# Moving VectorE's small SBUF operations of a kernel's first part to GpSimd, ScalarE and scalar operands

## The chip, the cores and the metric

The kernel runs on one core of a Trainium2 chip. The metric is the time of one execution on the device in microseconds (us). A core has engines that run their own instruction queues in order and wait for one another by semaphores: TensorE (PE, with its weight loads PEld), VectorE (DVE), ScalarE (ACT) and GpSimd (POOL); SyncE (SP) issues all of this kernel's DMA transfers from one queue.

## What is computed

```python
# attention over keys and values pooled by 8, 8 batches x 8 heads x 576 x 64
k_p = k.reshape(B, H, Sp, pool, D).mean(axis=3)
v_p = v.reshape(B, H, Sp, pool, D).mean(axis=3)
scores = scale * np.matmul(q, k_p.transpose(0, 1, 3, 2))
scores = scores - np.max(scores, axis=-1, keepdims=True)
attn = np.exp(scores)
attn = attn / (np.sum(attn, axis=-1, keepdims=True) + 1e-09)
x = np.matmul(attn, v_p)
# first layer, 4608 tokens, 512 -> 1024 -> 512
h = x @ w_in
e = np.exp(h - np.max(h, axis=-1, keepdims=True))
solu = h * (e / (np.sum(e, axis=-1, keepdims=True) + 1e-09))
mu = np.mean(solu, axis=-1, keepdims=True)
var = np.mean((solu - mu) ** 2, axis=-1, keepdims=True)
x = ((solu - mu) / np.sqrt(var + 1e-06) * g_ln) @ w_out
# second layer, 512 -> 2048 -> 512
h = x @ w_in2
y = (h * (1.0 / (1.0 + np.exp(-1.702 * h)))) @ w_out2
```

The weights arrive as 64-bit floats, two 32-bit words per number.

## The kernel before, in words

The work has two parts. The second part (from L1228) is the second layer, 12 blocks of 384 tokens, in an order written out by hand; the change does not touch it. The first part (L414 to L1226) does the attention and the first layer for 36 tiles of 128 tokens and, beside that, prepares all weights. Its order is made when the program is built: each piece of work is a "strand", a generator that yields operations (`V` DVE, `A` ACT, `G` POOL, `VG` POOL or DVE as the planner finds better, `T` matmuls, `D` a DMA on SP), and the planner (`Plan`, L173) takes next the operation that can start earliest by its own estimates, with a pull towards a strand's due time. The estimates are those of `cost` (L448): a DVE operation on up to 8 columns 70 ns (131 with a scalar operand), a POOL operation on two columns 202 ns, an ACT operation 93 ns and 0.83 ns per column. The planner's order is then fixed: each engine runs its queue in it and waits where an input is late.

The strands that matter here:

- `keys(b)` (L760), once per batch: the pooled keys `kp`, scaled into two halves of the block-diagonal tile `kbd` on DVE (L765).
- `values(b)` (L772): the pooled values; their largest magnitude gives a power of two as a scale (`largest`, L530, then `power_scale`, L555); `vx` holds the scaled values as two 16-bit halves. Then two one-column products `v_sc` of the scales, which POOL copies into the column `h_sc` of each tile.
- `largest` (L530) spreads a per-partition maximum over all partitions: `diag` = eye x maximum (DVE, 128 x 128), a matmul with ones, a maximum over the row. It runs 19 times: 8 times for the values, once each for `w_in`, `w_out` and `g_ln`, and 8 times for units of the second weights.
- `whole_scale` (L608) and `wide_scale` (L568) raise a power of two to the eighth power with one-column products `rc`, for `w_in` and `w_out` and for the 8 units of the second weights.
- `Quarter` and `values_of` (L578): the second weights, 16 chunks, turned from 64-bit to 32-bit floats on ACT, DVE (`raw`, a join of bits) and POOL (`w_f`), combined and split into two 16-bit halves, and stored to DRAM.
- `attention(t)` (L807), per tile: scores (`psx`), maximum `mx`, difference and exponential `e`, sum `rs`, then on DVE L851 adds 1e-9 and scales (8 columns, one per head) and L852 takes the reciprocal; `e` times `rs` on POOL (or DVE), split into `st` (ACT, then POOL), transposed by DMA, multiplied with the values (`psv`), split into `xT`.
- `Pair` (L895), two tiles of 128 tokens: `hidden` (L903) does the matmul with `w_in` (`psh`), the maximum, the exponential, `tt` = h x e with its sum `mean`, and the sum of squares `vs` on ACT. `norm` (L951) then has two columns per value, one for each tile: three DVE operations to the variance `v`, one POOL operation to the power -0.5 (`r`), four DVE operations to the factor `a` and the offset `mean`. ACT applies them to `tt`, ACT and POOL split the result into `zs`, and a DMA transposes it. `project` (L989) multiplies with `w_out` (`psy`), ACT copies `y`, and a DMA stores it.

The norm of the kernel before:

```python
yield V("scalar_tensor_tensor", out=q, in0=self.sm, scalar=1e-9, in1=self.ci, op0=ALU.add, op1=ALU.mult)
yield V("scalar_tensor_tensor", out=q, in0=q, scalar=tiny, in1=q, op0=ALU.mult, op1=ALU.mult)
yield V("scalar_tensor_tensor", out=v, in0=q, scalar=V_MOST, in1=self.vs, op0=ALU.min, op1=ALU.add)
yield G("tensor_tensor", out=r, in0=v, in1=minus_half, op=ALU.pow)
yield V("tensor_mul", q, r, r)
```

Of the kernel before, what the change touches and what calls it, by code (L numbers as in the profile page):

```python
# [12 lines left out]
AF = mybir.ActivationFunctionType  # L13
ALU = mybir.AluOpType
# [6 lines left out]
NPOOL = 8  # L21
SP = S // NPOOL
# [4 lines left out]
DF1 = 1024  # L27
# [49 lines left out]
TOP3 = 2.0 ** -29 * (1 - 2.0 ** -23)  # L77
A_TOP = 2.0 ** 14
LN_UP = 2.0 ** 10
SQ_DOWN = 1.0 / (LN_UP * math.sqrt(DF1))  # L80
V_MOST = 2.0 ** 100
Y_TOP = 2.0 ** 13
G_DOWN = 2.0 ** -22
TINY = 2.0 ** -100
# [88 lines left out]
class Plan:  # L173
# [30 lines left out]
    def drop(self, *tiles):  # L204
        for t in tiles:
            del self.ring_of[t.name]
# [71 lines left out]
def moe_kernel(ctx: ExitStack, tc: tile.TileContext, qT, kT, vT, w_in, w_out, g_ln, w2_in, w2_out, eye, outT):  # L278
# [27 lines left out]
    eye_t = const.tile([P, P], F32, name="eye_t")  # L306
# [107 lines left out]
    with ExitStack() as ph:  # L414
# [64 lines left out]
        def V(name, *args, **kw):  # L479
            return op(("dve",), name, args, kw)  # L480

        def G(name, *args, **kw):
            return op(("pool",), name, args, kw)
# [4 lines left out]
        def A(**kw):  # L488
            return op(("act",), "activation", (), kw)
# [40 lines left out]
        def largest(am, alln, least, early=True):  # L530


            if early:
                diag = yield New(sb, [P, P], F32, "diag0", "y", 2)
            else:
                diag = yield New(kv, [P, P], F32, "diag", bufs=1)
            yield V("tensor_scalar", out=diag, in0=eye_t, scalar1=am, scalar2=least, op0=ALU.mult, op1=ALU.max)
            yield there(diag)
            if early:
                ps = yield New(psy, [P, 2, YB], F32, "psy", "psy")  # L540
            else:
                ps = yield New(psv, [P, DM], F32, "psv", "psv")
            spread = ps[:, 0, :P] if early else ps[:, :P]
            yield T([(spread, ones, diag, True, True)])
            drop(diag)
            yield V("tensor_reduce", out=alln, in_=spread, axis=AX.X, op=ALU.max)
            drop(ps)

        def exponent(pw, alln):
            yield V(  # L550
# [17 lines left out]
        def wide_scale(alln, up, dn, there_now):  # L568
            pw, rc = s1("pw", 1, KM), s1("rc", 1, KM)
            yield from exponent(pw, alln)  # L570
            yield V("reciprocal", rc, pw)
            yield V("tensor_scalar_mul", up, rc, 2.0 ** -111)
            there_now.add((up.name, up.offset))
            yield V("tensor_mul", rc, pw, pw)
            yield V("tensor_mul", rc, rc, rc)
            yield V("scalar_tensor_tensor", out=dn, in0=rc, scalar=2.0 ** -8, in1=rc, op0=ALU.mult, op1=ALU.mult)

        def values_of(raw, up, dst, begun=None):  # L578

# [28 lines left out]
        def whole_scale(alln, up, dn):  # L608

            pw, rc = s1("pw", 1, KM), s1("rc", 1, KM)  # L610
            yield from exponent(pw, alln)
            yield V("reciprocal", rc, pw)
            yield V("tensor_mul", rc, rc, rc)
            yield V("tensor_mul", rc, rc, rc)
            yield V("scalar_tensor_tensor", out=up, in0=rc, scalar=2.0 ** 8, in1=rc, op0=ALU.mult, op1=ALU.mult)
            yield V("reciprocal", dn, up)

        def joined(raw, measured):
# [141 lines left out]
        def keys(b, due):  # L760
            kp = yield from pooled("k", b, kT, due)
            yield lambda: b < 2 or scored[last_tile(b - 2)]
            for j in range(2):
                r = slice(j * D64, (j + 1) * D64)
                yield V(  # L765
                    "tensor_scalar_mul", kbd[b % 2][r, :, j * SP : (j + 1) * SP], kp[r],
                    1.0 / (NPOOL * math.sqrt(D64)),
                )
            drop(kp)
            k_ready[b] = True  # L770

        def values(b, due):  # L772
            vp = yield from pooled("v", b, vT, due)
            am, alln, up, dn = s1("vam"), s1("v_all"), s1("v_up"), s1("v_dn")
            yield absmax_op(am, vp, axis=AX.XY)
            yield from largest(am, alln, TINY, b < 2)
            yield from power_scale("_v", alln, V_TOP, up, dn)
            yield lambda: b == 0 or v_ready[b - 1]
            yield A(
                out=vx[:, :, 0 : 2 * SP].rearrange("p a (r k) -> p a r k", r=2),  # L780
                in_=vp.unsqueeze(2).to_broadcast([P, NPAIR, 2, SP]), func=AF.Copy, scale=up,
            )
            yield V(
                "scalar_tensor_tensor", out=vx[:, :, 2 * SP : 3 * SP], in0=vp, scalar=up, in1=vx[:, :, 0:SP],
                op0=ALU.mult, op1=ALU.subtract,
            )
            drop(vp)
            yield lambda: b < 2 or valued[last_tile(b - 2)]
            yield D(vst[b % 2], vx.rearrange("p a k -> p (a k)"), turn=True)
            v_ready[b] = True  # L790
            yield w_in_done.over
            both = s1("v_sc", 2)
            yield V(
                "scalar_tensor_tensor", out=both[:, 0:1], in0=dn, scalar=1.0 / NPOOL, in1=w1i_dn, op0=ALU.mult,
                op1=ALU.mult,
            )
            yield V(
                "scalar_tensor_tensor", out=both[:, 1:2], in0=up, scalar=float(NPOOL), in1=w1i_up, op0=ALU.mult,
                op1=ALU.mult,
            )  # L800
            for t in range(NTILE):
                for o, n, tb in spans(t):
                    if tb == b:
                        yield G("tensor_copy", h_sc[o : o + n, t], both[o : o + n])
            h_ready[b] = True

        def attention(t):  # L807
# [40 lines left out]
                yield A(out=e, in_=e, func=AF.Exp)  # L848
            rs = s1("rs", H)
            yield V("tensor_reduce", out=rs, in_=e, axis=AX.X, op=ALU.add)  # L850
            yield V("tensor_scalar", out=rs, in0=rs, scalar1=1e-9, scalar2=1.0 / A_TOP, op0=ALU.add, op1=ALU.mult)  # L851
            yield V("reciprocal", rs, rs)  # L852
            yield VG("tensor_tensor", out=e, in0=e, in1=rs.unsqueeze(2).to_broadcast([P, H, SP]), op=ALU.mult)
            yield lambda: t < 2 or turned[t - 2]
# [40 lines left out]
        class Pair:  # L895
# [7 lines left out]
            def hidden(self, j):  # L903
# [10 lines left out]
                for k in range(KM):  # L914
# [26 lines left out]
                    accum_out=self.mean[:, s],  # L941
                )
                drop(ps)
                yield V("tensor_scalar_mul", self.mean[:, s], self.mean[:, s], -SQ_DOWN / DF1)
                yield A(
                    out=e, in_=tt, func=AF.Square, scale=SQ_DOWN, bias=self.mean[:, s], accum_out=self.vs[:, s]
                )
                drop(e)
                self.tt[j] = tt

            def norm(self):  # L951

                yield lambda: None not in self.tt
                a, v, r, q = (s1(n, 2) for n in ("a", "v", "r", "q"))
                self.a = a


                tiny = 1e-6 * DF1 * SQ_DOWN ** 2
                yield V("scalar_tensor_tensor", out=q, in0=self.sm, scalar=1e-9, in1=self.ci, op0=ALU.add, op1=ALU.mult)
                yield V("scalar_tensor_tensor", out=q, in0=q, scalar=tiny, in1=q, op0=ALU.mult, op1=ALU.mult)  # L960
                yield V("scalar_tensor_tensor", out=v, in0=q, scalar=V_MOST, in1=self.vs, op0=ALU.min, op1=ALU.add)
                yield G("tensor_tensor", out=r, in0=v, in1=minus_half, op=ALU.pow)
                yield V("tensor_mul", q, r, r)
                yield V("scalar_tensor_tensor", out=q, in0=q, scalar=-0.5, in1=v, op0=ALU.mult, op1=ALU.mult)
                yield V("scalar_tensor_tensor", out=a, in0=q, scalar=1.5, in1=r, op0=ALU.add, op1=ALU.mult)
                yield V(
                    "scalar_tensor_tensor", out=self.mean, in0=self.mean, scalar=1.0 / SQ_DOWN, in1=a, op0=ALU.mult,
                    op1=ALU.mult,
                )
                yield lambda: self.i == 0 or pairs[self.i - 1].zT is not None  # L970
                self.zT = yield New(sb, [P, 2 * K1, YB], F16, "zT", "zT", 2)
                for j in range(2):
                    s = slice(j, j + 1)
                    tt = self.tt[j]
                    yield A(out=tt, in_=tt, func=AF.Identity, scale=a[:, s], bias=self.mean[:, s])
                    zs = yield New(sb, [P, 2, DF1], F16, "zs", bufs=2)
                    yield A(out=zs[:, 0], in_=tt, func=AF.Copy)
                    yield VG("tensor_tensor", out=zs[:, 1], in0=tt, in1=zs[:, 0], op=ALU.subtract)
                    drop(tt)
                    yield D(self.zT[:, :, j * P : (j + 1) * P], zs.rearrange("p a c -> p (a c)"), turn=True)  # L980
                    drop(zs)
                yield w1o_done.over
                both = [start(self.project(h), self.due + LAG_PROJECT) for h in range(2)]
                yield until(*both)
                drop(self.zT)
# [488 lines left out]
```

## Time and profile before

| | before |
|---|---|
| median of 3 runs (lowest to highest) | 1301.56 us (1301.0 to 1302.12) |
| the profiled execution's own time, its span | 1298.91 us, 1297.1 us |
| PE busy in the span | 1160.6 us (89%) |
| DVE busy | 823.3 us (63%) |
| ACT busy | 753.0 us (58%) |
| POOL busy | 638.1 us (49%) |

Busy times are of the whole span; the two parts of the kernel load the engines differently, so they are read by stretch below. An operation's time runs from its start on the engine to its end and holds whatever it stands waiting for in between; idle time ahead of it, in which the engine waits for a semaphore, is counted by itself.

### The profile page before, as it was taken

To read this page: it belongs to the slowest core of one execution; us is meant where nothing else is said; L and a number is where in the kernel's file an instruction comes from. 1 tells how busy PE (TensorE), PEld (TensorE's weight loads), DVE (VectorE), ACT (ScalarE), POOL (GpSimd) and SP (SyncE) were. 2 spreads that over 40 slices of the span, in tenths; PEclk is the share of its full clock that TensorE was granted. 3 is DMA by queue.
4 is the path that set the end of the run, shared out by engine and by line. 5 is a ranking of instruction groups with operands and counts; after the bars stand their busy time and mean duration, and the time that the engine had idled before them with its cause. 6 is when DMAs were issued, how large, how long until landed. Compare 5 with 4: busy or idle time off the path is not lost.

```text
span 1297.1 us, 27516 instructions
## 1 busy us (share of the span) xinstructions
PE 1160.6 (89%) x11678; PEld 996.9 (77%) x11678; DVE 823.3 (63%) x1315; ACT 753.0 (58%) x1009; POOL 638.1 (49%) x541
## 2 busy tenths in 40 slices
PE   2677899888889989899999999999999999999998
PEld 2335566555555656588999999999999999999998
DVE  8999987698988685414454727364554637273633
ACT  6887767677677676435453725454453636364543
POOL 5875846677876585313341526152333415252431
PEclk9989899999899999999999999999999999999999
DMA  9979996987999649926010010101010100101000
GB/s 325 274 223 206 264 233 173 203 218 192 243 267 248 127 118 232 268 74 260 14 38 25 26 32 26 44 8 44 14 38 14 38 26 26 50 8 44 9 18 25
DMA packets 246523, 152.85 MB, mean 118 GB/s; under 512 B 163584, under 2 KB 226176, under 8 KB 244096
## 3 DMA queue, kind: packets, MB, share of 16 engines
q1 hardware_dynamic: 246400, 151.09, 44.0%
q8 instruction: 91, 1.49, 0.5%
q14 instruction: 32, 0.26, 0.1%
HBM read 77.66 MB, written 33.55 MB: 86 GB/s over the span
## 4 chain that ended last, share of the span: by engine, by line
PE 37%; DVE 29%; POOL 13%; ACT 11%; issue 7%; DMA 1%; SPq 1%; ACTq 0%; POOLq 0%; DVEq 0%
PE bank_a L1284 17%; PE bank_d L1284 7%; ACT w_g L1319 6%; DVE g L1331 5%; PE psy L501 5%; PE psh L501 5%; POOL w_g L333 3%; POOL w_g L332 3%; DVE raw L472 2%; POOL w_g L330 2%; PE bank_b L1284 2%; DVE q L472 2%; DVE tt L472 2%; POOL w_g L331 2%; DVE rs L472 2%
## 5 line engine op out<-in xcount | busy, mean ns | idle before, releaser
L1284 PEld LDWEIGHTS <-w2i 128*128 128x128 f16 x4032 | 334.7, 98 | 30.5 <-issue 30.3
L1284 PEld LDWEIGHTS <-w2o 128*128 128x128 f16 x4032 | 334.9, 98 | 8.2 <-issue 7.5
L1284 PE MATMUL bank_a<-ys,w2i 128*128 128x192 f16 x2304 | 213.7, 246 | 24.2 <-ACT c L1294 22.1
L330 POOL TENSOR_TENSOR w_g<-w_g 128x384 f32<-128x384 f32 x36 | 44.2, 1227 | 375.2 <-ACT w_g L1319 375.2
L501 PE MATMUL psh<-w1i,xT 128*128 128x512 f16 x864 | 211.5, 398 | 9.5 <-DVE rs L472 3.7
L501 PE MATMUL psy<-zT,w1o 128*128 128x256 f16 x1728 | 202.3, 277 | 7.4 <-ACT y L472 6.3
L1284 PE MATMUL bank_a<-g,w2o 128*128 128x192 f16 x2304 | 206.1, 246 | 1.1
L501 PEld LDWEIGHTS <-w1o 128*128 128x128 f16 x1728 | 171.1, 99 | 37.3 <-issue 9.7
L1331 DVE SCALAR_TENSOR_TENSOR g<-w_g,gu_b,g 128x1152 f16<-128x1152 f32 (+1 forms) x96 | 168.5, 1775 | 25.3 <-ACT g L1328 25.2
L501 PEld LDWEIGHTS <-xT 128*128 128x128 f16 x864 | 85.7, 102 | 109.5 <-issue 21.2
L1294 ACT ACTIVATE c<-bank_a 128x384 f32<-128x384 f32 x192 | 91.6, 484 | 111.9 <-PE bank_a L1284 110.2
L1328 ACT ACTIVATE g<-w_g,gu_b 128x1152 f16<-128x1152 f32 (+1 forms) x96 | 132.8, 1407 | 38.4 <-POOL w_g L333 38.0
L1297 DVE SCALAR_TENSOR_TENSOR c<-bank_d,c 128x384 f32<-128x384 f32 x96 | 53.3, 555 | 132.2 <-ACT c L1294 97.8
L472 POOL TENSOR_TENSOR zs<-tt,zs 128x1024 f16<-128x1024 f32 x36 | 77.3, 2147 | 78.2 <-ACT zs L472 78.0
L1284 PE MATMUL bank_d<-ys,w2i 128*128 128x192 f16 x1152 | 105.5, 247 | 0.0
L1284 PE MATMUL bank_d<-g,w2o 128*128 128x192 f16 x1152 | 102.5, 246 | 3.3 <-DVE g L1331 3.3
L1319 ACT ACTIVATE w_g<-c,ch_b 128x1536 f32<-128x1536 f32 x48 | 75.3, 1568 | 36.7 <-DVE c L1297 36.6
L1294 ACT ACTIVATE c<-bank_a,co_b 128x384 f32<-128x384 f32 x47 | 26.9, 573 | 108.5 <-PE bank_a L1284 108.5
L501 PE MATMUL psx<-kbd,qt 128*128 128x144 f32 (+1 forms) x320 | 50.0, 325 | 31.5 <-issue 14.6
L501 PEld LDWEIGHTS psx<-kbd,qt 128*128 128x128 f32 (+1 forms) x320 | 44.2, 206 | 36.9 <-issue 33.1
L472 POOL TENSOR_TENSOR lo<-w_f,hi 128x512 f16<-128x512 f32 (+1 forms) x48 | 64.6, 1364 | 12.3 <-ACT hi L472 7.6
L1297 DVE SCALAR_TENSOR_TENSOR c<-bank_b,c 128x384 f32<-128x384 f32 x48 | 26.7, 556 | 63.6 <-ACT c L1294 46.8
(181 smaller groups left out, 1761.7 us busy)
## 6 DMA issues: line engine op xcount, KB each, us to landing
raw<-w_out SPq DMA_DIRECT2D x12, 1024.0 KB, 6.9
raw<-w_in SPq DMA_DIRECT2D x10, 1024.0 KB, 9.0
half<-kT SPq DMA_DIRECT2D x16, 576.0 KB, 5.3
half<-vT SPq DMA_DIRECT2D x16, 576.0 KB, 5.6
qt<-qT SPq DMA_DIRECT2D x36, 256.0 KB, 3.3
y_dram<-y SPq DMA_DIRECT2D x36, 256.0 KB, 2.7
y<-y_dram SPq DMA_DIRECT2D x48, 192.0 KB, 3.3
outT<-c SPq DMA_DIRECT2D x48, 192.0 KB, 1.9
```

What stands on the lines that cost most here:

```text
L330: eng.tensor_tensor(out=w[:, 1], in0=q[:, Q12], in1=q[:, Q11], op=ALU.subtract)
L331: eng.tensor_tensor(out=w[:, 2], in0=q[:, Q22], in1=w[:, 1], op=ALU.subtract)
L332: eng.tensor_tensor(out=w[:, 0], in0=q[:, Q22], in1=q[:, Q12], op=ALU.subtract)
L333: eng.tensor_tensor(out=w[:, 3], in0=q[:, Q21], in1=w[:, 2], op=ALU.subtract)
L472: getattr(eng, name)(*args, **kw)
L501: nc.tensor.matmul(*p[:3], start=p[3], stop=p[4])
L1284: nc.tensor.matmul(bank[:, q], self.weight(p, q, kk, w), self.data(p, kk, i), start=(first and q == 0 and kk == 0 and w == 0 and i == 0), ...
L1294: nc.scalar.activation(out=self.c[:, i], in_=bank, func=AF.Copy, scale=self.scale)
L1297: nc.vector.scalar_tensor_tensor(out=self.c[:, i], in0=bank, scalar=self.scale, in1=self.c[:, i], op0=ALU.mult, op1=ALU.add)
L1319: nc.scalar.activation(out=self.w[:, 0:4], in_=self.c, func=AF.Gelu_apprx_sigmoid, scale=self.ch)
L1328: nc.scalar.activation(out=self.g[:, 0, s], in_=self.w[:, s], func=AF.Copy, scale=self.gu)
L1331: nc.vector.scalar_tensor_tensor(out=self.g[:, 1, s], in0=self.w[:, s], scalar=self.gu, in1=self.g[:, 0, s], op0=ALU.mult, op1=ALU.subtract,)
```

## The change

It rewrites small operations of the first part, in six places:

1. `largest`: `diag` is made by ACT, and the lower limit `least` is applied to the result by a new one-column DVE operation.
2. `wide_scale` and `whole_scale`: products of a one-column tile with itself take the second factor as a scalar operand.
3. `keys`: `kbd` is written by ACT.
4. `values`: the scale products `v_sc` take scalar operands, and the second is limited on both sides by a third operation.
5. `attention`: ACT adds and scales `rs`; the reciprocal stays on DVE.
6. `Pair`: the square is taken without a scale, and the norm's ten operations all run on POOL, with other constants.

```diff
-            yield V("tensor_scalar", out=diag, in0=eye_t, scalar1=am, scalar2=least, op0=ALU.mult, op1=ALU.max)
+            yield A(out=diag, in_=eye_t, func=AF.Copy, scale=am)
...
             yield V("tensor_reduce", out=alln, in_=spread, axis=AX.X, op=ALU.max)
             drop(ps)
+            yield V("tensor_scalar_max", alln, alln, least)
...
-            yield V("tensor_mul", rc, pw, pw)
-            yield V("tensor_mul", rc, rc, rc)
-            yield V("scalar_tensor_tensor", out=dn, in0=rc, scalar=2.0 ** -8, in1=rc, op0=ALU.mult, op1=ALU.mult)
+            yield V("tensor_scalar_mul", rc, pw, pw)
+            yield V("tensor_scalar_mul", rc, rc, rc)
+            yield V("tensor_scalar", out=dn, in0=rc, scalar1=rc, scalar2=2.0 ** -8, op0=ALU.mult, op1=ALU.mult)
...
-            yield V("tensor_mul", rc, rc, rc)
-            yield V("tensor_mul", rc, rc, rc)
-            yield V("scalar_tensor_tensor", out=up, in0=rc, scalar=2.0 ** 8, in1=rc, op0=ALU.mult, op1=ALU.mult)
+            yield V("tensor_scalar_mul", rc, rc, rc)
+            yield V("tensor_scalar_mul", rc, rc, rc)
+            yield V("tensor_scalar", out=up, in0=rc, scalar1=rc, scalar2=2.0 ** 8, op0=ALU.mult, op1=ALU.mult)
...
-                yield V(
-                    "tensor_scalar_mul", kbd[b % 2][r, :, j * SP : (j + 1) * SP], kp[r],
-                    1.0 / (NPOOL * math.sqrt(D64)),
+                yield A(
+                    out=kbd[b % 2][r, :, j * SP : (j + 1) * SP], in_=kp[r], func=AF.Copy,
+                    scale=1.0 / (NPOOL * math.sqrt(D64)),
                 )
...
-            yield V(
-                "scalar_tensor_tensor", out=both[:, 0:1], in0=dn, scalar=1.0 / NPOOL, in1=w1i_dn, op0=ALU.mult,
-                op1=ALU.mult,
-            )
-            yield V(
-                "scalar_tensor_tensor", out=both[:, 1:2], in0=up, scalar=float(NPOOL), in1=w1i_up, op0=ALU.mult,
-                op1=ALU.mult,
-            )
+            c, ci = both[:, 0:1], both[:, 1:2]
+            yield V("tensor_scalar", out=c, in0=dn, scalar1=1.0 / NPOOL, scalar2=w1i_dn, op0=ALU.mult, op1=ALU.mult)
+            yield V("tensor_scalar", out=ci, in0=up, scalar1=w1i_up, scalar2=CI_LEAST, op0=ALU.mult, op1=ALU.max)
+            yield V("tensor_scalar_min", ci, ci, CI_MOST)
...
-            yield V("tensor_scalar", out=rs, in0=rs, scalar1=1e-9, scalar2=1.0 / A_TOP, op0=ALU.add, op1=ALU.mult)
+            yield A(out=rs, in_=rs, func=AF.Copy, scale=1.0 / A_TOP, bias=1e-9 / A_TOP)
             yield V("reciprocal", rs, rs)
...
-                yield V("scalar_tensor_tensor", out=q, in0=self.sm, scalar=1e-9, in1=self.ci, op0=ALU.add, op1=ALU.mult)
-                yield V("scalar_tensor_tensor", out=q, in0=q, scalar=tiny, in1=q, op0=ALU.mult, op1=ALU.mult)
-                yield V("scalar_tensor_tensor", out=v, in0=q, scalar=V_MOST, in1=self.vs, op0=ALU.min, op1=ALU.add)
+                yield G("tensor_scalar", out=q, in0=self.sm, scalar1=1e-9, scalar2=e0, op0=ALU.add, op1=ALU.mult)
+                yield G("tensor_tensor", out=q, in0=q, in1=self.ci, op=ALU.mult)
+                yield G("tensor_tensor", out=q, in0=q, in1=q, op=ALU.mult)
+                yield G("tensor_tensor", out=v, in0=q, in1=self.vs, op=ALU.add)
                 yield G("tensor_tensor", out=r, in0=v, in1=minus_half, op=ALU.pow)
-                yield V("tensor_mul", q, r, r)
-                yield V("scalar_tensor_tensor", out=q, in0=q, scalar=-0.5, in1=v, op0=ALU.mult, op1=ALU.mult)
-                yield V("scalar_tensor_tensor", out=a, in0=q, scalar=1.5, in1=r, op0=ALU.add, op1=ALU.mult)
-                yield V(
-                    "scalar_tensor_tensor", out=self.mean, in0=self.mean, scalar=1.0 / SQ_DOWN, in1=a, op0=ALU.mult,
-                    op1=ALU.mult,
-                )
+                yield G("tensor_tensor", out=q, in0=r, in1=r, op=ALU.mult)
+                yield G("tensor_tensor", out=q, in0=q, in1=v, op=ALU.mult)
+                yield G("tensor_scalar", out=q, in0=q, scalar1=-0.5 * k, scalar2=1.5 * k, op0=ALU.mult, op1=ALU.add)
+                yield G("tensor_tensor", out=a, in0=q, in1=r, op=ALU.mult)
+                yield G("tensor_tensor", out=self.mean, in0=self.mean, in1=a, op=ALU.mult)
```

## Rows read from the trace of the kernel before

**Rows 1.** The page's slices: busy tenths in 40 equal slices of the span.

```profile
PE   2677899888889989899999999999999999999998
DVE  8999987698988685414454727364554637273633
```

**Rows 2.** Busy time by stretch: us, then PE, PEld, DVE, ACT, POOL (x instructions), PEclk, DMA share, GB/s.

```profile
100.00:150.00 50.00, 40.16 (x308) 26.26 (x307) 49.51 (x89) 38.99 (x56) 35.58 (x32) 0.91 1.09 232
50.00:500.00 450.00, 380.26 (x2870) 253.61 (x2869) 393.69 (x720) 335.43 (x492) 321.65 (x299) 0.94 0.86 209
500.00:590.00 90.00, 80.87 (x649) 61.65 (x648) 27.25 (x62) 39.50 (x52) 23.63 (x16) 0.96 0.68 185
590.00:1297.00 707.00, 676.24 (x8043) 666.24 (x8040) 359.02 (x466) 343.05 (x405) 259.79 (x188) 1.00 0.11 37
```

**Rows 3.** The chain of waits, 50 to 500 us, shares by engine, tile and line.

```profile
by line: PE psh L501 10.3%; issue 10.0%; DVE raw L472 6.3%; DVE tt L472 5.6%; DVE q L472 5.5%; PE psy L501 5.0%; DVE rs L472 3.9%; DVE e L472 3.7%; DVE hmx L472 3.1%; DVE xT L472 2.6%; DVE mx L472 2.4%; DVE rc L472 2.4%; POOL e L472 2.3%; D
```

**Rows 4.** Groups, DVE, 50 to 500 us: out<-in, shape, count | busy us, mean ns | idle before.

```profile
L472 DVE TENSOR_SCALAR rs<-rs 128x8 f32<-128x8 f32 x32 | 12.8, 401 | 0.4
L472 DVE SCALAR_TENSOR_TENSOR q<-hsm,h_sc 128x2 f32<-128x2 f32 x15 | 9.1, 609 | 0.0
L472 DVE SCALAR_TENSOR_TENSOR a<-q,r 128x2 f32<-128x2 f32 x15 | 9.1, 607 | 0.3
L472 DVE TENSOR_TENSOR q<-r 128x2 f32<-128x2 f32 x15 | 8.7, 581 | 1.4 <-POOL r L472 1.4
L472 DVE TENSOR_TENSOR rc<-pw 128x1 f32<-128x1 f32 x8 | 8.5, 1067 | 0.2
L472 DVE SCALAR_TENSOR_TENSOR q<-q 128x2 f32<-128x2 f32 x15 | 8.4, 563 | 0.1
L472 DVE SCALAR_TENSOR_TENSOR q<-q,v 128x2 f32<-128x2 f32 x15 | 7.6, 504 | 0.4
L472 DVE TENSOR_SCALAR diag<-eye_t,vam 128x128 f32<-128x128 f32 x7 | 7.0, 995 | 0.0
L472 DVE TENSOR_SCALAR diag<-eye_t,w2a 128x128 f32<-128x128 f32 x8 | 6.5, 813 | 0.1
L472 DVE SCALAR_TENSOR_TENSOR v<-q,vs 128x2 f32<-128x2 f32 x15 | 6.5, 431 | 0.5
L472 DVE TENSOR_SCALAR kbd<-kp 64x288 f32<-64x288 f32 x12 | 6.2, 518 | 0.2
L472 DVE SCALAR_TENSOR_TENSOR mean<-mean,a 128x2 f32<-128x2 f32 x15 | 5.2, 345 | 0.3
L472 DVE TENSOR_TENSOR rc<-rc 128x1 f32<-128x1 f32 x10 | 4.9, 492 | 0.2
```

**Rows 5.** Timeline near 260 us, DVE and POOL: start us, us, engine, operation.

```profile
259.91 0.15 DVE L472 TENSOR_SCALAR w2i_up<-rc 128x1 f32<-128x1 f32 x1
260.10 2.13 DVE L472 TENSOR_TENSOR rc<-pw 128x1 f32<-128x1 f32 x1
262.26 0.16 DVE L472 TENSOR_TENSOR rc<-rc 128x1 f32<-128x1 f32 x1
...
260.08 2.13 POOL L472 TENSOR_TENSOR zs<-tt,zs 128x1024 f16<-128x1024 f32 x1 [0.57 <-ACT zs L472]
```

**Rows 6.** Groups, POOL, 50 to 500 us, the operations on two columns.

```profile
L472 POOL TENSOR_TENSOR r<-v,half_power 128x2 f32<-128x2 f32 x15 | 11.4, 761 | 5.6 <-DVE v L472 5.2
L472 POOL COPY h_sc<-v_sc 128x2 f32<-128x2 f32 (+1 forms) x35 | 6.5, 228 | 3.8 <-DVE v_sc L472 3.6
```

**Rows 7.** Groups, ACT, 0 to 620 us, its narrowest forms and a wider one.

```profile
L472 ACT ACTIVATE e<-e 128x576 f32<-128x576 f32 x35 | 23.7, 676 | 10.3 <-DVE e L472 10.0
...
L472 ACT ACTIVATE e<-psx,mx 128x72 f32<-128x72 f32 x8 | 1.8, 336 | 2.7 <-DVE mx L472 2.7
```

**Rows 8.** Waits, 0 to 600 us: us in total, times, longest us.

```profile
POOL zs L472 <- ACT zs L472: 78.0, 26, 12.2
...
SPq L493 <- POOL zs L472: 46.9, 14, 10.1
```

More of the change, by code (lines that the diff above doesn't have):

```diff
@@ L79 @@
 LN_UP = 2.0 ** 10
-SQ_DOWN = 1.0 / (LN_UP * math.sqrt(DF1))
-V_MOST = 2.0 ** 100
+CI_LEAST, CI_MOST = 2.0 ** -50, 2.0 ** 40
 Y_TOP = 2.0 ** 13
@@ L943, in hidden @@
                 drop(ps)
-                yield V("tensor_scalar_mul", self.mean[:, s], self.mean[:, s], -SQ_DOWN / DF1)
-                yield A(
-                    out=e, in_=tt, func=AF.Square, scale=SQ_DOWN, bias=self.mean[:, s], accum_out=self.vs[:, s]
-                )
+                yield V("tensor_scalar_mul", self.mean[:, s], self.mean[:, s], -1.0 / DF1)
+                yield A(out=e, in_=tt, func=AF.Square, bias=self.mean[:, s], accum_out=self.vs[:, s])
                 drop(e)
@@ L955, in norm @@
                 self.a = a
-                tiny = 1e-6 * DF1 * SQ_DOWN ** 2
-                yield V("scalar_tensor_tensor", out=q, in0=self.sm, scalar=1e-9, in1=self.ci, op0=ALU.add, op1=ALU.mult)
-                yield V("scalar_tensor_tensor", out=q, in0=q, scalar=tiny, in1=q, op0=ALU.mult, op1=ALU.mult)
-                yield V("scalar_tensor_tensor", out=v, in0=q, scalar=V_MOST, in1=self.vs, op0=ALU.min, op1=ALU.add)
-                yield G("tensor_tensor", out=r, in0=v, in1=minus_half, op=ALU.pow)
-                yield V("tensor_mul", q, r, r)
-                yield V("scalar_tensor_tensor", out=q, in0=q, scalar=-0.5, in1=v, op0=ALU.mult, op1=ALU.mult)
-                yield V("scalar_tensor_tensor", out=a, in0=q, scalar=1.5, in1=r, op0=ALU.add, op1=ALU.mult)
-                yield V(
-                    "scalar_tensor_tensor", out=self.mean, in0=self.mean, scalar=1.0 / SQ_DOWN, in1=a, op0=ALU.mult,
-                    op1=ALU.mult,
-                )
+                e0 = NPOOL * math.sqrt(1e-6 * DF1)
+                k = LN_UP * math.sqrt(DF1)
+                yield G("tensor_scalar", out=q, in0=self.sm, scalar1=1e-9, scalar2=e0, op0=ALU.add, op1=ALU.mult)
+                yield G("tensor_tensor", out=q, in0=q, in1=self.ci, op=ALU.mult)
+                yield G("tensor_tensor", out=q, in0=q, in1=q, op=ALU.mult)
+                yield G("tensor_tensor", out=v, in0=q, in1=self.vs, op=ALU.add)
+                yield G("tensor_tensor", out=r, in0=v, in1=minus_half, op=ALU.pow)
+                yield G("tensor_tensor", out=q, in0=r, in1=r, op=ALU.mult)
[3 more added lines that the diff above has]
+                yield G("tensor_tensor", out=self.mean, in0=self.mean, in1=a, op=ALU.mult)
                 yield lambda: self.i == 0 or pairs[self.i - 1].zT is not None
```

## The prediction, made before the result was known

> **What bounds the kernel now.** I first read the page's slices for where the time lies: VectorE (DVE) is busy at nine tenths or more in the first slices and at seven to nine tenths until about 500 us, where it falls to three to six tenths; TensorE (PE) stands at nine from about 590 us on [rows 1]. The busy time by stretch puts numbers on that [rows 2]. From 50 to 500 us, the part that the change touches, DVE is busy for 393.7 of 450 us (87%), PE 380.3 (85%), ScalarE (ACT) 335.4 (75%), GpSimd (POOL) 321.7 (71%); in 100 to 150 us DVE has half a microsecond free. From 500 to 590 us DVE is down to 27.3 of 90 us and PE holds 80.9 (90%): there PE empties its list of output projections. After 590 us PE is at 676.2 of 707 us (96%), and none of the edited lines runs there. So the first 450 us are where it is decided, DVE is the fullest engine in them, and PE is close behind.
>
> The chain of waits says the same: in this stretch it runs through many DVE tiles, and small ones stand among the large. `q`, two numbers per partition, has 5.5% of the chain, `rs` 3.9%, `rc`, one number per partition, 2.4% [rows 3]. An operation on two columns should not weigh that much. The groups by form show why it does: the `q`, `a`, `v` and `mean` steps of a pair's norm take 345 to 609 ns each, the `rc` product over one column 1067 ns [rows 4]. The timeline of one of them shows what they spend it on: a one-column scale takes 0.15 us, the next operation, a one-column product of two tiles, 2.13 us, and the next one of its kind 0.16 us; the 2.13 us are, start and end, those of POOL's `zs` subtraction [rows 5]. So these operations do no work for most of their time: they stand while POOL works, and DVE's queue stands behind them. **The term to price is that standing.**
>
> **What leaves DVE, 50 to 500 us** [rows 4]. Norm, seven operations per pair, 15 pairs: 9.1 + 8.4 + 6.5 + 8.7 + 7.6 + 9.1 + 5.2 = 54.6 us, all to POOL. `rs`, the sum's scaling per tile of 128 tokens: 12.8 us to ACT. `diag`: 7.0 + 6.5 = 13.5 us to ACT. `kbd`: 6.2 us to ACT. The `rc` products stay on DVE with a one-column scalar operand: 18 of them cost 8.5 + 4.9 = 13.4 us now; at the 0.15 us of the one-column scale with an immediate [rows 5] they cost 2.7, a gain of 10.7. The new `max` after the spread's reduction (one per `diag`, 15 x 0.15 = 2.3 us) and the split of the `v_sc` pair into three are set against what the scale products `v_sc` and `dn` stop standing: taken as even. Together 54.6 + 12.8 + 13.5 + 6.2 + 10.7 = 97.8 us. DVE falls from 393.7 to about 296 us of work for the same stretch, 66% of it. What still can stand behind POOL is the bit join `raw`, `vx` and the few `e` products that fall to DVE; they are not edited.
>
> **What POOL takes on.** Per pair ten operations in place of one, so 9 x 15 = 135 new ones. The trace has no plain two-input operation on two columns on POOL. Nearest is the two-column copy `h_sc`, 228 ns, as small, but with one input; the other end is the power `r`, 761 ns, two inputs, but another function [rows 6]. I take 228 (seven of the nine are adds or products of two columns, nearer in work to a copy than to a power): 135 x 0.228 = 30.8 us, POOL 321.7 + 30.8 = 352 us. The upper end is 102.7 us, POOL 424. The lower end is nothing, if all of them fall into POOL's idle waits. The GPSIMD Engine Reference of the Trainium skill ("Performance versus the Vector engine") speaks against the move: an elementwise operation of two inputs takes about twice as long there as on DVE. By it, an estimate, twice the 0.16 us of an unhindered DVE operation gives 135 x 0.32 = 43 us, POOL 365, the same verdict as below.
>
> **What ACT takes on.** No operation of eight columns is there to read. From 72 columns at 336 ns and 576 columns at 676 ns [rows 7] each column costs 0.675 ns, which gives 0.29 us for 8 columns, 0.37 for 128, 0.48 for 288: 32 x 0.29 + 15 x 0.37 + 12 x 0.48 = 20.6 us. ACT comes to 356 us. Bounds: nothing, where the operation falls into an idle stretch of ACT, and 59 x 0.676 = 40 us, were each as long as the 576-column one; neither makes ACT the fullest.
>
> **The waits that come and go.** A pair's norm crosses to POOL and back now (`v` to `r`, `r` to `q`); after, it is one run of POOL operations, begun when ACT's square sum is there, and only ACT's scaling of `tt` waits for its end. Queued behind it on POOL are the `e`, `st` and `zs` products and the second weights' combinations; ACT's `st` waits for the first, the queue that issues transfers (SP) for the others. It already waits 46.9 us for `zs`, and POOL itself 78.0 us for ACT's `zs` [rows 8], so POOL has idle time there that the new operations can use. `rs` gets two new crossings per tile: DVE's sum, ACT's scaling, DVE's reciprocal. Everything on DVE behind the reciprocal waits if ACT is late. I cost the crossings at nothing, because DVE now has 450 - 296 = 154 us free; where that cover is gone they are the second rival. The order of every queue is laid anew by the planner, transfers on SP included, since `cost` gives each moved operation another price; no row tells which way this goes. One misplaced operation costs up to the longest single wait shown, 12.2 us [rows 8], in either direction, and I carry that in the range.
>
> **The sum.** With DVE at 296, POOL 352 and ACT 356, the fullest engine is PE with its unchanged 380.3 us. Had it no more room than DVE had (87%), the stretch would last 380.3 / 0.875 = 435 us, 15 us less. Where DVE does not crowd it, from 500 to 590 us, PE holds 80.9 / 90 = 90% [rows 2]: 380.3 / 0.899 = 423 us, **27 us less**. I take this one, since the row shows the same code with DVE out of the way. The chain bears the size out: `q`, all of it moved, has 5.5% of 450 us = 25 us on it, and `rc` 11 us. The most: PE's granted clock is 0.94 there against 1.00 after 590 us [rows 2]; were the gaps that go with the low clock to close, 380.3 x 0.94 / 0.899 = 398 us, 52 us less. The 90 us behind are bound by PE, the rest is not touched: nothing. The profiled execution took 1298.91 us with a span of 1297.1; the median of the runs is 1301.56, 2.65 above it. 1298.91 - 27 = 1271.9 profiled, 1274.5 as a median.
>
> **Rivals.**
> 1. *POOL becomes the bound (slower).* Place: the ten dependent operations of a norm in POOL's in-order queue. For it: POOL at 352 of a 423 us stretch is already 83% full, each operation reads the one before, and the only two-input operation of two columns there takes 761 ns. Against: that one is a power. At 761 ns POOL holds 424 us, at 90% filling 472 us, 22 us longer: 1323.6. It decides from (0.9 x 450 - 321.7) / 135 = 0.62 us per operation.
> 2. *The crossings eat half.* ACT's 492 instructions average 335.4 / 492 = 0.68 us; an `rs` scaling that arrives behind one of them and takes 0.29 itself holds DVE's queue for about 1 us, 32 times: 32 us of new DVE idle, as DVE `rs` waiting for ACT `rs`. With PE fullest, perhaps half of the gain goes: 1288. For it: POOL already waits for `rs` on the way to `e`. Against: DVE has 154 us free.
> 3. *No change.* The gaps on PE are set by the order of its queue and by transfers; DVE's work goes and PE's gaps stay, 10% of the chain being already issue [rows 3]: 1301. Against: small DVE operations are links of the chain, not beside it.
>
> **How the numbers follow.** A measurement of this kernel tells about 0.2% (2.6 us) from no change. Forecast (1248 to 1287): 0.60. Rival 2 (1287 to 1299): 0.19. Rival 3: 0.08. Rival 1 and any other slower order: 0.13. Faster is 0.60 + 0.19 = 0.79. The range reaches from the 52 us bound, 1249.6, rounded out to 1248, up to no change, 1302; most of rival 1 stays outside.
>
> **What would show it.** Right: DVE near 296 us of work before PE's final projections, no moved `q`, `a`, `rs` on it, `rc` at about 0.15 us, POOL's two-column operations at 0.2 to 0.3 us, and PE's share in the stretch near 90%. Wrong: two-column POOL operations at 0.6 us or more, long waits of DVE `rs` for ACT, or a PE share still at 85%; any run above 1302 refutes the balance of engines as the reason.

## The result, and the profile after

The changed kernel takes 1267.15 us (median of 4 runs, 1265.34 to 1271.79) against 1301.64 before: a ratio of 0.974, 95% interval [0.9721, 0.9759], 34.5 us less. That is inside the range and on the side that was forecast; the point, 1274.5, was 7 us too high. The profiled execution has a span of 1264.3 us, 32.8 less than before. Times below are medians as well; one of the four runs of the last kernel, at 2389.08 us nearly twice as long as its other three, is left out of its numbers.

First the page's slices after, as in [rows 1]:

```profile
PE   2768998899999999699999999999999999999998
DVE  8799787567787552317364544546372737364543
```

DVE is at nine tenths in two slices where it was in six, and PE comes to its nines earlier. Then the busy time by stretch, with the columns of [rows 2]:

```profile
50.00:500.00 450.00, 403.91 (x3156) 272.42 (x3155) 326.77 (x603) 366.37 (x579) 357.09 (x452) 0.97 0.92 222
500.00:590.00 90.00, 75.92 (x753) 68.41 (x752) 31.39 (x51) 40.92 (x49) 30.18 (x30) 0.95 0.67 203
```

PE is busy for 403.9 of 450 us, 89.8%, where it was 380.3; it did 3156 matmuls in the stretch instead of 2870. DVE went from 393.7 to 326.8 us, POOL from 321.7 to 357.1, ACT from 335.4 to 366.4. What the part gained shows in its last projection matmul, the `psy` group of either kernel, before and then after (count, shortest/median/longest ns, first and last start):

```profile
L501 PE MATMUL psy<-zT,w1o x1728: 269/273/421, 109.9 to 586.9; 128*128 128x256 f16 x192
```

```profile
L500 PE MATMUL psy<-zT,w1o x1728: 269/273/421, 114.0 to 552.5; 128*128 128x256 f16 x192
```

It starts at 552.5 instead of 586.9 us, 34.4 us earlier: the whole gain lies in the first part. The groups that answer to [rows 4], of VectorE after, 50 to 500 us (`q`, `a`, `v` and the norm's `mean` no longer run there, nor the scaling of `rs`, `diag` and `kbd`):

```profile
L471 DVE SCALAR_TENSOR_TENSOR raw<-raw 128x512 int32<-128x512 int32 x40 | 40.6, 1026 | 2.6 <-ACT raw L471 2.3
...
L471 DVE TENSOR_TENSOR e<-e,rs 128x576 f32<-128x576 f32 x7 | 9.8, 1404 | 0.1
L471 DVE RECIPROCAL rs<-rs 128x8 f32<-128x8 f32 x32 | 6.3, 197 | 4.7 <-ACT rs L471 4.4
...
L471 DVE TENSOR_SCALAR rc<-rc 128x1 f32<-128x1 f32 x10 | 2.1, 206 | 0.2
L471 DVE TENSOR_SCALAR rc<-pw 128x1 f32<-128x1 f32 x8 | 1.7, 212 | 0.2
```

The `rc` products, with a scalar operand, take 0.21 us where they took 1.07 and 0.49: they stand no longer. The join `raw` does as before (1026 ns, 1064 in the kernel before). The crossing of `rs` costs DVE 4.4 us of waiting in the stretch, not 32. The groups that answer to [rows 6], POOL after, two columns, 50 to 500 us:

```profile
L471 POOL TENSOR_TENSOR r<-v,half_power 128x2 f32<-128x2 f32 x17 | 13.9, 819 | 0.7
...
L471 POOL TENSOR_SCALAR q<-hsm 128x2 f32<-128x2 f32 x17 | 4.8, 282 | 1.4
L471 POOL TENSOR_TENSOR q<-q 128x2 f32<-128x2 f32 x17 | 4.7, 278 | 0.7
...
L471 POOL TENSOR_TENSOR q<-r 128x2 f32<-128x2 f32 x17 | 3.3, 195 | 0.7
```

The nine operations that are new on POOL take 195 to 282 ns each; only the power is slow. And ACT's, as [rows 7] were to price them:

```profile
L471 ACT ACTIVATE rs<-rs 128x8 f32<-128x8 f32 x32 | 6.4, 200 | 6.5 <-DVE rs L471 6.4
L471 ACT ACTIVATE kbd<-kp 64x288 f32<-64x288 f32 x12 | 5.3, 438 | 0.2
L471 ACT ACTIVATE diag<-eye_t,w2a 128x128 f32<-128x128 f32 x8 | 3.2, 394 | 0.0
```

Last the chain of waits after, 50 to 500 us, beside [rows 3]:

```profile
by line: POOL w_f L471 11.0%; PE psh L500 10.3%; PE psy L500 7.8%; POOL lo L471 7.4%; issue 7.0%; ACT he L471 3.9%; DMA raw<-w_out 3.6%; POOL st L471 3.5%; POOL zs L471 3.1%; ACT tt L471 2.9%; POOL q L471 2.4%; POOL e L471 2.3%; DMA aT<-st 
```

No DVE tile is among its thirteen first any more, where there were nine; POOL has taken that place with `w_f`, `lo`, `st`, `zs`. The stretch is now POOL's and PE's.

### The profile page after: what moved, and what is told of

Its sections match the earlier page's. It is cut to its first block, busy times and chain, and to the rows that moved or that the text cites. A ratio compares the mean times of both kernels' runs of the same rounds, so it can differ in the third digit from the quotient of the medians.

```text
span 1264.3 us, 27579 instructions
## 1 busy us (share of the span) xinstructions
PE 1145.6 (91%) x11678; PEld 991.2 (78%) x11678; DVE 735.5 (58%) x1150; ACT 766.7 (61%) x1073; POOL 667.8 (53%) x699
## 4 chain that ended last, share of the span: by engine, by line
PE 37%; POOL 23%; DVE 13%; ACT 13%; issue 6%; DMA 6%; SPq 0%; ACTq 0%; POOLq 0%; DVEq 0%
PE bank_a L1278 18%; PE bank_d L1278 7%; ACT w_g L1313 6%; DVE g L1325 5%; PE psy L500 4%; PE psh L500 4%; POOL w_f L471 4%; POOL w_g L332 3%; POOL w_g L331 3%; POOL lo L471 3%; PE bank_b L1278 3%; POOL w_g L329 2%; POOL w_g L330 2%; POOL zs L471 2%; DMA aT<-st 1%
## 5 line engine op out<-in xcount | busy, mean ns | idle before, releaser
L500 PE MATMUL psy<-zT,w1o 128*128 128x256 f16 x1728 | 200.5, 275 | 18.1 <-ACT y L471 10.5
L500 PE MATMUL psh<-w1i,xT 128*128 128x512 f16 x864 | 203.8, 388 | 1.8 <-DVE mean L471 1.6
L1291 DVE SCALAR_TENSOR_TENSOR c<-bank_d,c 128x384 f32<-128x384 f32 x96 | 53.3, 555 | 132.4 <-ACT c L1288 97.8
L1313 ACT ACTIVATE w_g<-c,ch_b 128x1536 f32<-128x1536 f32 x48 | 75.3, 1568 | 36.8 <-DVE c L1291 36.7
L500 PE MATMUL psx<-kbd,qt 128*128 128x144 f32 (+1 forms) x320 | 47.4, 311 | 30.4 <-issue 13.1
L471 DVE TENSOR_REDUCE hmx<-psh 128x1 f32<-128x1024 f32 x36 | 43.7, 1215 | 41.7 <-PE psh L500 41.6
```

The costliest lines, as they stand in the source:

```text
L471: getattr(eng, name)(*args, **kw)
L500: nc.tensor.matmul(*p[:3], start=p[3], stop=p[4])
L1291: nc.vector.scalar_tensor_tensor(out=self.c[:, i], in0=bank, scalar=self.scale, in1=self.c[:, i], op0=ALU.mult, op1=ALU.add)
L1313: nc.scalar.activation(out=self.w[:, 0:4], in_=self.c, func=AF.Gelu_apprx_sigmoid, scale=self.ch)
```

## The experiments

Each ratio below is that to the kernel before as measured beside the run on the same chip, with its 95% interval in brackets.

The theory (A): small DVE operations that read two tiles, or several columns, stand while POOL works, and DVE's queue behind them; the time that this queue gets back is the gain. The rivals: the planner's new order (B), the norm's shorter way without crossings, that is without results handed from one engine to another (C), the price of the `rs` crossings (D), any small operation standing whatever its operands (E), and chains rather than queue time (F).

**Order and operations apart.** The change does two things: it changes instructions, and through the planner's prices the order of every queue. A small helper separates them; the planner is given one operation, and others are issued in its place:

```diff
+        def as_(planned, *real):
+
+            def emit(engine):
+                for o in real:
+                    o.emit(o.engines[0])
+
+            planned.emit = emit
+            return planned
...
-            yield V("tensor_scalar", out=rs, in0=rs, scalar1=1e-9, scalar2=1.0 / A_TOP, op0=ALU.add, op1=ALU.mult)
+            yield as_(
+                V("tensor_scalar", out=rs, in0=rs, scalar1=1e-9, scalar2=1.0 / A_TOP, op0=ALU.add, op1=ALU.mult),
+                A(out=rs, in_=rs, func=AF.Copy, scale=1.0 / A_TOP, bias=1e-9 / A_TOP),
+            )
...
```

In the traces PE's 11678 matmuls and SP's transfers then come in exactly the order of the kernel whose plan is kept. *All of the change, order of the kernel before:*

> All of the change's instructions, in the order of the kernel before: the planner sees the old operations, with their old engines and prices, and each is then issued in its new form. Theory A (DVE no longer stands behind POOL; the work that leaves it is the gain): most of the 34 us come although the order is the old one, 1266 to 1282, DVE busy about 65 to 90 us less in 50 to 500 us. Rival B (the gain comes from the new order that the planner laid, by luck or by its better estimates): at least two thirds of it go, 1290 or more.

1278.46 us against 1301.38, ratio 0.9831 [0.9787, 0.9875]: 22.9 us less, inside A's range, with DVE 83.8 us less busy in 50 to 500 us. The stretch, with the columns of [rows 2], and the group on DVE that waits for ACT's `rs`:

```profile
50.00:500.00 450.00, 393.74 (x3048) 263.51 (x3048) 309.88 (x587) 360.86 (x569) 358.15 (x447) 0.96 0.92 226
L473 DVE RECIPROCAL rs<-rs 128x8 f32<-128x8 f32 x32 | 6.4, 201 | 15.0 <-ACT rs L473 15.0
```

PE fills 87.5% here, not yet 89.8, and the crossing of `rs` costs DVE 15.0 us of waiting where the changed kernel has 4.4. *The mirror, order after and operations before:*

> The mirror of the run before: the order that the planner lays for the changed kernel, but with the old instructions (norm, rs, diag, kbd on DVE, products of two tiles). Theory A: the gain is gone, 1288 to 1315, and the small DVE operations take 0.3 to 1.1 us each again. Rival B: 1280 or less.

1296.7 us, ratio 0.9964 [0.9947, 0.9981]: 4.7 us less. The operations stand again; the groups of DVE in this run, 50 to 500 us:

```profile
L473 DVE TENSOR_SCALAR rs<-rs 128x8 f32<-128x8 f32 x33 | 19.3, 583 | 0.2
L473 DVE TENSOR_TENSOR q<-r 128x2 f32<-128x2 f32 x15 | 11.2, 745 | 3.3 <-POOL r L473 3.2
...
L473 DVE TENSOR_TENSOR rc<-pw 128x1 f32<-128x1 f32 x8 | 5.7, 708 | 0.2
```

So the operations alone are worth 22.9 us in the old order (16 to 28 by the interval), the order alone 4.7 us with the old operations, and the two together 34. About two thirds are A; B has a share. How large an order's share can be by luck was tried with one planner constant moved. A first try

> The changed kernel with one planner constant moved a little (PULL 950 for 900), which changes no operation, only the order. It measures what the order by itself is worth: within 4 us of 1267 if orders are alike, 8 or more away if the 5 to 11 us that the new order brought can be luck.

gave 1267.31 us, but its trace shows every queue in the order of the changed kernel: the constant moved nothing, and the run says only that the changed kernel repeats. Another constant did move the order on every engine:

```diff
-    LAG = {"pe": 197, "dve": 150, "act": 160, "pool": 75, "dma": 950}
+    LAG = {"pe": 197, "dve": 150, "act": 180, "pool": 75, "dma": 950}
```

> The changed kernel with the planner's estimate of ScalarE's hand-over at 180 ns for 160: the same operations in a different order on every engine. If an order is worth little by itself: 1267 within 4 us. If orders laid with the same prices scatter by as much as the 5 to 11 us that the new order brought: 1272 or more, or 1262 or less.

> The kernel before with the same shift of the planner's estimate, so the old operations in another order. Within 4 us of 1301 if orders are alike; 1297 or less, or 1305 or more, if they scatter as much as the new order gained with the old operations (4.7 us).

With the changed operations 1266.87 us, ratio 0.9745 [0.972, 0.977], as without the shift; with the old ones 1297.18 against 1299.94, ratio 0.9975 [0.9961, 0.9988]. One more order of each kind moved the time by 0.3 and 2.8 us. The 4.7 us of the mirror run is therefore not far from what any other order may give; the step from 1278.5 to 1267.2 with the new operations, 11.3 us, is more than either shift showed, which speaks for the planner fitting the order to the new operations. DVE's wait for `rs`, 15.0 us in the old order and 4.4 in the new, is one thing that it fitted. But two other orders are too few to settle it, and both shifts are smaller than the change's own: counted in the traces, PE's queue holds another tile's matmul in 426 and 702 places after the shifts and in 1396 after the change.

**The parts.** Both in the order of the kernel before:

> Only the norm's seven operations go to POOL, in the order of the kernel before. Theory A: gain in proportion to the DVE time that goes, 54.6 of 97.8 us, so about 19 of 34 us, 1278 to 1288. Rival C (the norm's shorter way without crossings is the whole gain): 1265 to 1275. Rival B: 1295 to 1305.

> The change without the norm, in the order of the kernel before: rs, diag, kbd to ACT, one-column products with scalar operands. Theory A: about 15 of 34 us, 1282 to 1292. Rival C: no gain, 1297 to 1303. Rival D (the new crossings of rs to ACT and back cost more than the standing): slower than 1303, with long waits of DVE rs for ACT rs.

The norm alone: 1287.11 us, ratio 0.9892 [0.9871, 0.9912], 14.3 us less. All but the norm: 1290.9, ratio 0.9925 [0.9909, 0.9941], 10.5 us less. They add up to 24.8 us, and both at once gave 22.9. C falls, the norm is not the whole, and D falls, the crossings do not eat the gain, although DVE waits 9.7 us for ACT's `rs` in the second of these runs. DVE's busy totals in the profiles put both on one price: 823.3 us before, 772.0 with the norm moved, 783.6 with the rest: 51.3 us for 14.3 and 39.7 for 10.5, 0.26 to 0.28 us of time per us of DVE. Both at once come a little lower, 100.7 us for 22.9, or 0.23.

**Standing, or the work itself.** The norm stays on DVE, but by columns, each operation with scalar operands; seven operations on two columns become fourteen on one, issued in place of the planned seven:

```diff
-                yield V("scalar_tensor_tensor", out=q, in0=self.sm, scalar=1e-9, in1=self.ci, op0=ALU.add, op1=ALU.mult)
...
+                yield as_(
+                    V("scalar_tensor_tensor", out=q, in0=self.sm, scalar=1e-9, in1=self.ci, op0=ALU.add, op1=ALU.mult),
+                    V("tensor_scalar", out=q[:, 0 : 1], in0=self.sm[:, 0 : 1], scalar1=1e-9, scalar2=self.ci[:, 0 : 1], op0=ALU.add, op1=ALU.mult),
+                    V("tensor_scalar", out=q[:, 1 : 2], in0=self.sm[:, 1 : 2], scalar1=1e-9, scalar2=self.ci[:, 1 : 2], op0=ALU.add, op1=ALU.mult),
+                )
...
```

> As the run of all but the norm, order of the kernel before, and the norm stays on DVE, but one column at a time with scalar operands: 14 operations in place of 7, none of which reads two tiles. Theory A in its form 'a second tile from SBUF makes DVE stand behind POOL': every norm operation takes 0.15 to 0.25 us and never 0.3 or more; DVE loses 10 to 20 us per stretch although it runs twice as many instructions, 1283 to 1289. Rival E (any small DVE operation stands while POOL works): the operations still average 0.3 us or more, DVE gains nothing or grows, 1291 or more.

1276.82 us, ratio 0.9817 [0.9787, 0.9847]: 14 us under the run of all but the norm, better than expected, and level with 1278.46, all of the change in the same order, where POOL has the norm. The norm's crossings to POOL and back are all still there, so C falls once more. The two runs' groups on DVE, 50 to 500 us, first all but the norm, with the norm's old two-column operations:

```profile
L473 DVE SCALAR_TENSOR_TENSOR q<-q 128x2 f32<-128x2 f32 x16 | 13.8, 859 | 0.2
L473 DVE TENSOR_TENSOR q<-r 128x2 f32<-128x2 f32 x16 | 11.3, 704 | 4.2 <-POOL r L473 4.2
L473 DVE SCALAR_TENSOR_TENSOR q<-hsm,h_sc 128x2 f32<-128x2 f32 x16 | 11.0, 690 | 0.0
L473 DVE SCALAR_TENSOR_TENSOR a<-q,r 128x2 f32<-128x2 f32 x16 | 10.7, 670 | 0.3
L473 DVE SCALAR_TENSOR_TENSOR q<-q,v 128x2 f32<-128x2 f32 x16 | 8.6, 538 | 0.4
L473 DVE SCALAR_TENSOR_TENSOR v<-q,vs 128x2 f32<-128x2 f32 x16 | 7.0, 435 | 0.6
L473 DVE SCALAR_TENSOR_TENSOR mean<-mean,a 128x2 f32<-128x2 f32 x15 | 6.0, 403 | 0.4
```

and by columns:

```profile
L473 DVE TENSOR_SCALAR v<-q,vs 128x1 f32<-128x1 f32 x32 | 5.6, 206 | 0.8 <-ACT he L473 0.8
L473 DVE TENSOR_SCALAR q<-r 128x1 f32<-128x1 f32 x32 | 5.3, 206 | 2.8 <-POOL r L473 2.8
L473 DVE TENSOR_SCALAR a<-q,r 128x1 f32<-128x1 f32 x32 | 5.3, 206 | 0.0
L473 DVE TENSOR_SCALAR mean<-mean,a 128x1 f32<-128x1 f32 x32 | 5.2, 205 | 0.0
L473 DVE TENSOR_SCALAR q<-q,v 128x1 f32<-128x1 f32 x32 | 5.2, 205 | 0.0
L473 DVE TENSOR_SCALAR q<-hsm,h_sc 128x1 f32<-128x1 f32 x32 | 5.2, 202 | 0.0
L473 DVE TENSOR_SCALAR q<-q 128x1 f32<-128x1 f32 x32 | 5.0, 199 | 0.0
```

Twice the operations take 36.8 us where half as many took 68.4. Every group averages 199 to 206 ns; none stands. One by one the traces say the same: in the kernel before, 49 of the norm's 105 operations in the stretch take more than 0.3 us, and each of the 49 starts inside a POOL instruction and ends 13 to 23 ns after the end of one (nine others start inside one and do not stand). By columns the longest of 224 takes 215 ns, although 164 of them start inside a POOL instruction. E falls: it is what the operation reads, not that it is small or that POOL is busy.

The Trainium skill ("SBUF — State Buffer", section "SBUF: two separate sides") has an exclusive lock between GpSimd and those DVE instructions that run in a two-port mode, or take two SBUF inputs while GpSimd reads SBUF; the one that starts later waits until the other ends. The trace agrees: the two-column operations read two tiles and end with a POOL instruction, the one-column ones read one tile and scalars and do not wait. That one column stays out of the two-port mode is taken from their not waiting; no run shows it apart.

DVE's total falls by 28.2 us, 783.6 to 755.4, for these 14 us: 0.50 us of time per us of DVE, about twice the price of the parts. So the price is no constant. Shorter norms, which others wait for, may add to the queue's own time here; no run separates the two.

**The time put back.** A sum over a constant tile, which nobody waits for, 72 times, behind each `rs` reciprocal and each scaling of a tile's `mean`:

```diff
-            yield V("reciprocal", rs, rs)
+            yield as_(V("reciprocal", rs, rs), V("reciprocal", rs, rs), V("tensor_reduce", out=pad_out, in_=pad, axis=AX.X, op=ALU.add))
...
```

> The changed kernel in its own order, with 72 operations on DVE added that nobody waits for (a sum over a constant tile of 768 columns, about 0.8 us each, about 60 us in all) behind each rs reciprocal and each scaling of the mean. Nothing crosses engines, nothing stands. Theory A in its form 'the time that DVE's queue is taken is what counts, 0.27 us per us': 1278 to 1290. Rival F (what counts is the shorter chains and the crossings, DVE has room): 1265 to 1272.

1283.56 us, ratio 0.9869 [0.9838, 0.9899]: 16.3 us more than the changed kernel's 1267.31 beside it on the same chip. The added group, 0 to 590 us:

```profile
L473 DVE TENSOR_REDUCE pad_out<-pad 128x1 f32<-128x768 f32 x72 | 66.4, 923 | 0.0
```

DVE's total rises from 735.5 to 794.5 us, 59 us: 0.28 us of time per us, the same price as when the parts took it away. F falls as the whole account: nothing crosses here, and the queue's time alone costs.

**A version that beats both.** If standing is what costs, the norm need not load POOL, which has the chain after the change. The changed kernel with the norm by columns, in the planner's own order, and then with more of the large products kept on POOL (`SPARE`, the nanoseconds by which DVE must be the earlier one to be given such a product, goes from 3000 to 6000):

> The changed kernel with the norm on DVE by columns and the planner free to order it. Theory A: POOL is relieved of some 31 us, DVE gets about 42 us of operations that do not stand; at 0.27 us per us of DVE, 1270 to 1282, unless POOL, at 79% of the stretch, is the next limit, which would give 1255 to 1266.

> The kernel with the norm on DVE by columns, and the planner keeping more of the large products on POOL (SPARE 6000 for 3000), since POOL has room again and the e products on DVE read two tiles and stand. If their standing still matters: 1250 to 1260. If it is an order like others: 1257 to 1270.

1261.68 us, ratio 0.9697 [0.9667, 0.9728], and 1256.83 us, ratio 0.965 [0.962, 0.9681]. The stretch of 50 to 500 us of the two, with the columns of [rows 2]:

```profile
50.00:500.00 450.00, 404.72 (x3149) 273.08 (x3148) 343.66 (x833) 366.36 (x578) 333.29 (x308) 0.96 0.97 234
```

```profile
50.00:500.00 450.00, 409.10 (x3198) 276.97 (x3195) 338.92 (x829) 367.85 (x580) 335.70 (x312) 0.97 0.99 235
```

POOL has 333.3 us in place of 357.1, DVE 343.7 in place of 326.8, and PE fills 90 to 91%. The first beats the changed kernel by 5.6 us: its slowest run, 1264.97 us, lies under the fastest of the changed kernel on the same chip, 1265.47, though the intervals of the two ratios overlap by a thousandth. It fell where the expectation had put it if POOL was the next limit. The second is 10.0 us under the changed kernel in its other order (1266.87 us, same chip), with intervals well apart. The step from the first to the second is not established, as their intervals overlap, and it is not the standing of the `e` products on DVE: the first has only two of them in the stretch, at half the 1424 ns that the five of the kernel before average, and the second none.

```profile
L473 DVE TENSOR_TENSOR e<-e,rs 128x576 f32<-128x576 f32 x2 | 1.5, 748 | 0.0
```

## Why the prediction was right

- *Standing is the term to price*: shown. By columns the norm stays on DVE and gains as much as on POOL; with the old operations it stands in the new order too. Of DVE's slices, said to be at seven to nine tenths until 500 us, two are at six; nothing hangs on it.
- *97.8 us leave DVE, 296 remain*: in the old order, with all of the change, DVE's total falls by 823.3 - 722.6 = 100.7 us. In the changed kernel it falls by 87.8: the planner gave DVE seven `e` products instead of five, two `w_f` instead of one, and a `zs`; they average 1.4, 1.9 and 2.7 us. The 326.8 us in the stretch also hold work that came earlier into it.
- *POOL at 228 ns an operation*: the nine groups measure 195 to 282 ns; 357.1 us in the stretch against 352 forecast. The end at 761 ns, and rival 1 with it, is refuted: the power is slow, not two inputs. POOL is the slower engine for them, 195 to 282 ns against 0.16 us of an unhindered DVE operation, and by columns on DVE they did as well in the old order and 5.6 us better in the planner's. The Trainium skill (GPSIMD Engine Reference, "Performance versus the Vector engine") has POOL about two times slower on elementwise operations of two inputs; the trace agrees on which engine is slower, and the 0.32 us worked out from that factor, an estimate, lies above every group measured.
- *ACT*: `rs` 200 ns against 290 forecast, `kbd` 438 against 480, `diag` 394 against 370. Rival 2 asked for some 32 us of DVE waiting for ACT's `rs`; the trace has 4.4. But the crossings were costed at nothing because DVE has room, and in the old order, with even more room on DVE, the wait is 15.0 us, half of what rival 2 asked for: that it came so low is the new order's doing.
- *PE at 90% gives 27 us*: PE fills 89.8% in the changed kernel, but not by the operations alone; in the old order it fills 87.5%, the lower share of the prediction's sum, and the gain is 22.9 us. What the point lacked is the clock: it took PE's work at the granted clock of 0.94, and the clock of the stretch is 0.96 in the old order and 0.97 in the new. With it the same sum gives 380.3 x 0.94 / 0.96 / 0.875 = 426 us, 24 us less than 450, and 380.3 x 0.94 / 0.97 / 0.898 = 410 us, 40 us less. Against the 40, PE waits in the tail, which the prediction took to be unchanged: 42.3 of 53 us busy from 500 us on, with a wait of 7.4 us for the transfer of `zT`. The bound of 52 us had the clock; the point did not. These splits are worked out, not measured by runs of their own.
- *The order*: left open in the prediction with 12 us either way. It brought 4.7 us with the old operations and 11.3 with the new ones; without it the result would have been 1278.5, inside the range too, 4 us on the other side of the point. So the range does not owe its hit to luck, but the side of the point on which the time fell was not foreseen.

## What to carry to other kernels

A small operation with a duration many times that of its neighbours is worth one look at the other engine's timeline: if its end falls with the end of a GpSimd instruction, it is waiting inside its own duration, and a busy share does not tell that from work. Before moving such operations to another engine, try giving them scalar operands and one column at a time: twice the instructions took half the time here. Where a planner lays the order, measure a change of operations with the old order pinned as well, or the order's share is taken for the change's.

## What was not expected of the hardware

- Standing is not a fixed price. With `rs`, `diag`, `kbd` and `rc` out of the way and the same order, the norm's operations stood longer than before: `q<-q` 859 ns against 563 in [rows 4], the seven together 68.4 us for 16 pairs against 54.6 for 15. Two partial cures therefore need not add up as their rows do.
- A one-column operation on DVE with a scalar from a tile takes 199 to 214 ns, with an immediate 142 to 154 in the changed kernel: the 0.15 us of the prediction held for immediates alone.
- ACT does eight columns in 200 ns, less than a line through its 72 and 576 column forms gives (290): the 72-column form also carries a bias from a tile, which was not tried apart.
- Two tiles are enough to make an operation stand, even on one column (`rc`, 1067 ns in the kernel before), and one tile with eight columns can be (the scaling of `rs`, 401 ns there). But the reciprocal over the same eight columns averages 200 ns there, its longest 204: it never stands. Why these two differ stays open.
